# Low bits of all weight tiles by a 16-bit shift on VectorE, the first chunk's remainders on POOL, four rebiases on ScalarE, and a new order for the first part

## The chip, the cores and the metric

One core of one Trainium2 chip. The metric is the time of one execution in device microseconds (us). A core has TensorE (PE in the profile; PEld is its weight load), VectorE (DVE), ScalarE (ACT), GpSimd (POOL) and SyncE (SP, which issues nearly all transfers). Each engine works through its own queue in order and waits on semaphores for the others.

## The reference

A block attention followed by a gated feed-forward layer, in fp32.

```python
# 8 batches, 8 heads, 512 local and 32 global tokens, head size 64
s_g = scale * q_g @ [k_g, k_l].T;  out_g = softmax(s_g) @ [v_g, v_l]
# a local token sees the 32 global keys and local keys within 32 places
out_l = softmax([scale * q_l @ k_g.T, masked scale * q_l @ k_l.T]) @ [v_g, v_l]
x = concat(out_g, out_l), heads side by side          # 8 * 544 rows of 512
xn = x / sqrt(mean(x * x) + 1e-6) * rms_g
g = xn @ w_gate;  val = xn @ w_val                    # 512 x 1536 each
out = (g * sigmoid(g) * val) @ w_out                  # 1536 x 512
```

The kernel's weights arrive as float64: the host passes each as pairs of 32-bit words, a low and a high one, and the kernel makes fp32 of them on the chip.

## The kernel before

The tokens go through in nine chunks: chunks 0 to 7 are the 512 local rows of a batch, chunk 8 the 256 global rows. A matmul in full precision is made of three fp16 products: a value is split into a high half (its rounding to fp16) and a low half (the remainder), and high by high, high by low and low by high are summed. Chunks 0 and 1 compute attention unit by unit (two heads each, units 0 to 3 for chunk 0 and 4 to 7 for chunk 1); from chunk 2 on the weights are used in a folded form that chunk 1 writes to device memory.

Everything up to chunk 1's first product of the layer is the "first part": all of chunk 0, chunk 1's attention, and the preparation of all weights. Its order is written out by hand in the string `ORDER`, a list of jobs. A job is a letter, a number and sometimes an index; it issues its instructions on its engines, and the order of the list is the order of each engine's queue. What comes later (chunks 1 to 8) is ordered by loops with slots.

The jobs that matter here, with the number of the unit, tile or f behind the letter:

- Attention of a unit: `L` and `V` load, `S` scores (TensorE), `M` masked least value (VectorE, from PSUM), `E` exponentials (ScalarE), `T` transposes (TensorE), `C` copies (ScalarE), `A` values (TensorE), `R` reciprocal and `X` division (VectorE), `Q` squares (ScalarE), `Z` their sums (VectorE).
- Norm of a chunk: `N` 13 small steps (VectorE), `D` four diagonal factors `dg` (VectorE, L888), `U` transposed and scaled rows (TensorE), `H` their high half (ScalarE), `Y` their low half (VectorE).
- Weight tile i (0 to 11 are tiles of w_gate and w_val, 12 to 17 of w_out, two blocks f each): `W` load of two raw tiles `wr`, `m` rebias of the high word (VectorE for the tiles of `MULT_V`, else ScalarE), `s` shift by 3 (VectorE), then the three low bits: `l` (VectorE, ORed into the tile) or, for the tiles of `LOW_A`, `k` (ScalarE, into the low half of the raw high word), `g` sign and, after `k`, these bits (VectorE), `q` squares (ScalarE). `p` and `e` make scales of a group of tiles (TensorE, VectorE), `a` is the high half (ScalarE), `d` the low half (VectorE). `K0` to `K2` make the scales of w_out, which `a12` and the later ones need.
- Layer of chunk 0, block f: `I` four products (TensorE), `B` tanh (ScalarE), `b` gate and `h` inner product (VectorE, from PSUM), `c` the high half of the result (ScalarE), `r` its remainder (`low` in `first_chunk`). `Oi.j` are the output products of blocks 2i and 2i+1 for rows j, `o` the store. `J`, `j`, `u` fold a tile for the later chunks.

Since the banks of PSUM for I's two halves are single, I of block f+1 starts when `b` (and for its second half `h`) of block f is done.

Of the kernel before, what the change touches and what calls it, by code (L numbers as in the profile page):

```python
# [11 lines left out]
F16 = mybir.dt.float16  # L12
BF16 = mybir.dt.bfloat16
I32 = mybir.dt.int32
U32 = mybir.dt.uint32
I16 = mybir.dt.int16
AF = mybir.ActivationFunctionType
ALU = mybir.AluOpType
AX = mybir.AxisListType
# [3 lines left out]
P = 128  # L23
# [15 lines left out]

ORDER = """  # L40

L0 L1 L2 L3 W0 W1 V0 V1 S0 z0 V2 V3 z1 M0.0 W2 M0.1 S1 E0.0 W3 z2 W4 E0.1 T0.0 W5 M1.0 z3 W6
M1.1 S2 C0.0 L4 R0 E1.0 z4 L5 T0.1 m0 W7 E1.1 M2.0 T1.0 z5 M2.1 S3 C0.1 R1 s0 E2.1 m1 T1.1 M3.0
E2.0 M3.1 A0 z6 E3.1 R2 s1 l0 V4 C1.0 C1.1 X0 T2.0 E3.0 g0 A1 l1 Q0 T2.1 C2.0 V5 X1 T3.0 C2.1
R3 Z0 Q1 T3.1 g1 q0 A2 Z1 q1 p0 X2 C3.0 p1 C3.1 e0 Q2 A3 m2 e1 Z2 a0 s2 X3 k2 d0 m3 Q3 g2 m4 Z3
q2 s3 N0.0 k3 s4 N0.1 N0.2 N0.3 N0.4 N0.5 N0.6 N0.7 N0.8 a1 g3 k4 N0.9 d1 W8 S4 N0.10 N0.11
N0.12 q3 D0 L6 g4 U0.0 m5 M4.0 U0.1 H0.0 s5 q4 Y0.0 U0.2 M4.1 H0.1 k5 Y0.1 U0.3 I0.00 H0.2 g5
H0.3 I0.10 Y0.2 q5 W9 Y0.3 p2 m6 m7 I0.01 e2 k6 s6 I0.11 s7 l7 p3 B0 a2 b0 W10 e3 a3 I1.00 W11
h0 a4 d2 I1.01 c0 a5 d4 I1.10 B1 r0 m8 I1.11 b1 d5 m9 I2.00 h1 m10 d3 I2.10 c1 k9 g6 I2.01 r1
I2.11 g7 B2 q6 b2 W12 s9 q7 I3.00 h2 g9 c2 I3.10 k10 r2 I3.01 s8 m11 I3.11 B3 l8 k11 p4 b3 g8  # L50
I4.00 W13 e4 q8 I4.01 h3 a6 s11 I4.10 s10 B4 d6 q9 I4.11 c3 b4 a7 r3 I5.00 h4 d7 c4 I5.10 E4.1
r4 I5.01 g10 I5.11 g11 B5 q10 p5 b5 q11 m12 I6.00 h5 m13 e5 I6.10 c5 s12 a8 r5 I6.01 l12 k13
I6.11 d8 p6 B6 g12 a9 b6 W14 q12 d9 I7.00 W15 E4.0 h6 I7.01 e6 c6 s13 a10 I7.10 r6 B7 g13 m14
I7.11 b7 W16 q13 d10 I8.00 m15 h7 I8.01 s14 c7 s15 a11 I8.10 r7 l15 B8 m16 I8.11 b8 k14 s16
I9.00 h8 g15 I9.10 c8 g14 k16 W17 I9.01 r8 I9.11 d11 B9 q14 T4.0 b9 T4.1 g16 q15 I10.00 h9 m17
S5 R4 q16 s17 I10.01 L7 M5.0 c9 I10.10 M5.1 B10 C4.0 r9 C4.1 I10.11 b10 E5.1 l17 I11.00 E5.0
h10 A4 g17 c10 I11.01 R5 q17 X4 V6 r10 Q4 I11.10 K0 B11 Z4 b11 K1 I11.11 K2 a12 T5.0 h11 T5.1
S6 C5.0 d12 C5.1 c11 A5 M6.0 a13 O0.0 M6.1 V7 E6.0 X5 O0.1 d13 Q5 T6.0 E6.1 r11 O0.2 Z5 O0.3
a14 R6 C6.0 T6.1 d14 S7 C6.1 O1.0 a15 M7.0 M7.1 E7.0 O1.1 d15 O1.2 E7.1 T7.0 O1.3 a16 R7 T7.1
d16 A6 O2.0 X6 C7.0 C7.1 Q6 A7 a17 Z6 O2.1 X7 d17 Q7 O2.2 Z7 G J0 j0 u0 O2.3 N1.0 N1.1 N1.2  # L60
N1.3 N1.4 O3.0 N1.5 N1.6 N1.7 N1.8 N1.9 N1.10 O3.1 N1.11 N1.12 D1 J1 j1 u1 J2 j2 u2 O3.2 O3.3
O4.0 O4.1 O4.2 O4.3 O5.0 O5.1 o0 U1.0 o1 O5.2 H1.0 Y1.0 U1.1 o2 O5.3 H1.1 Y1.1 U1.2 o3 U1.3
H1.2 Y1.2 H1.3 Y1.3
"""


# [1 line left out]
def attention_moe_kernel(  # L68
# [17 lines left out]
    nc = tc.nc  # L86
# [20 lines left out]
    def f32(ap):  # L107
        return ap.bitcast(F32)
# [28 lines left out]
    ends = con.tile([P, 1], I32, tag="ends", name="ends")  # L137
# [16 lines left out]
    def sub(eng, dst, a, b):  # L154
        if eng == "V":
            nc.vector.tensor_tensor(dst, a, b, ALU.subtract)
        else:
            nc.gpsimd.tensor_tensor(dst, a, b, ALU.subtract)  # L158
# [31 lines left out]
    g2 = con.tile([P, 2], F32, tag="g2", name="g2")  # L190
# [47 lines left out]
    def convert(i):  # L238

        src = w_in[i] if i < NF else w_out[i - NF]  # L240
        raws = []
        t = []

        def load():
            for w in range(2):
                raw = raw_tile(RAW[i], f"wr{i}{w}")
                QW.dma_start(raw, src[:, w, :].bitcast(I32))
                r = raw.rearrange("p (n t) -> p n t", t=2)
                raws.append((slice(w * 512, (w + 1) * 512), r[:, :, 0], r[:, :, 1], raw))

        def rebias():

            t.append(
                xg.rearrange("p k n -> p (k n)").bitcast(I32)
                if i == NF - 1
                else raw_tile("wo" if i >= NF else "wf", f"w{i}t")
            )
            t32[i] = f32(t[0])
            for c, _, hi, _ in raws:
                if i in MULT_V:  # L260
                    nc.vector.tensor_single_scalar(f32(t[0][:, c]), f32(hi), REBIAS, ALU.mult)
                else:
                    nc.scalar.mul(f32(t[0][:, c]), f32(hi), REBIAS)

        def shift():
            nc.vector.tensor_single_scalar(t[0], t[0], 3, ALU.logical_shift_left)

        def three():

            for _, lo, _, raw in raws:  # L270
                half = raw.bitcast(I16).rearrange("p (n t) -> p n t", t=4)
                nc.scalar.activation(  # L272
                    half[:, :, 2],
                    lo.bitcast(U32),
                    AF.Copy,
                    bias=-0.5 + 7.5 * 2.0**-18,
                    scale=(1 - 2.0**-18) * 2.0**-29,
                )

        def low():  # L280
            for c, lo, _, _ in raws:
                nc.vector.scalar_tensor_tensor(
                    t[0][:, c], lo, 29, t[0][:, c], ALU.logical_shift_right, ALU.bitwise_or
                )

        def sign():

            keep = ends if i in LOW_A else -(1 << 30)
            for c, _, hi, _ in raws:
                nc.vector.scalar_tensor_tensor(  # L290
                    t[0][:, c], hi, keep, t[0][:, c], ALU.bitwise_and, ALU.bitwise_or
                )
# [993 lines left out]
    def first_chunk():  # L1286
        ch = chunks[0]
        ps, ts = {}, {}
# [348 lines left out]
```

## Time and profile before

| | |
|---|---|
| median of 3 runs | 933.66 us (933.59 to 934.74) |
| profiled execution, first to last instruction | 930.2 us |
| what lies around it, by the median | 3.5 us |
| busy: PE, VectorE, ScalarE, POOL | 893.9, 634.0, 495.4, 253.8 us |
| chunk 1's first product | 170.73 us |
| TensorE idle up to there | 28.8 us |

The page gives no separate time for the profiled execution beside its span; the median stands for it. A row of a timeline is the start, the duration, the engine, the line, the instruction and its operands (out<-in), a count where like rows follow each other, and in brackets the idle time before it with what ended it. The durations of one engine's instructions overlap a little, so costs are taken from start to start.

### The profile page before, as it was taken

The page shows a single profiled execution, that of the slowest core. Times are in us where ns is not written, and L with a number is a line of the kernel's source. Part 1 is how long each engine was busy: PE and PEld are TensorE (multiplying, and loading weights), DVE is VectorE, ACT ScalarE, POOL GpSimd, SP SyncE. Part 2 cuts the span into 40 slices and gives each one's busy share as a digit, 9 for nine tenths or more (in the row PEclk, how much of TensorE's full clock was granted, in tenths as well). Part 3 has the DMA queues.
Part 4 walks back from the last instruction along what each step waited for, and adds up shares of the span by engine and source line. Part 5 has one row for each costly group of instructions (what it writes and reads, how often), then busy time and mean ns, then how long its engine had stood idle before and what let it go on. Part 6 is the DMA issues. An engine that isn't in the chain of part 4 may idle for free.

```text
span 930.2 us, 26398 instructions
## 1 busy us (share of the span) xinstructions
PE 893.9 (96%) x11028; PEld 612.2 (66%) x11028; DVE 634.0 (68%) x1603; ACT 495.4 (53%) x1232; POOL 253.8 (27%) x219
## 2 busy tenths in 40 slices
PE   5489999999999999999999999999999999999998
PEld 4444455545447885688648874788568865886584
DVE  6999987887884588557775679357846774664331
ACT  6999994555443564456344655356445732543131
POOL 0000000142423262334332353236233432332020
PEclk9699999999999999999999999999999999999999
DMA  9972533686449854495609771685349632787000
GB/s 352 407 288 96 159 120 115 209 265 198 144 119 320 282 180 147 133 299 169 213 24 279 242 238 43 200 279 184 139 136 297 190 95 79 248 273 238 35 1 23
DMA packets 83495, 173.40 MB, mean 186 GB/s; under 512 B 6705, under 2 KB 25393, under 8 KB 83377
## 3 DMA queue, kind: packets, MB, share of 16 engines
q1 hardware_dynamic: 82944, 171.40, 56.1%
q8 instruction: 86, 1.41, 0.6%
q10 hardware_dynamic: 432, 0.33, 0.1%
q14 instruction: 33, 0.26, 0.1%
HBM read 150.21 MB, written 21.50 MB: 185 GB/s over the span
## 4 chain that ended last, share of the span: by engine, by line
PE 82%; DVE 8%; DMA 4%; ACT 3%; issue 1%; POOL 1%; ACTq 0%; DVEq 0%; POOLq 0%
PE pq L1108 36%; PE po L1266 23%; PE p L1205 9%; PE a L708 4%; PE po L1333 3%; PE s L665 3%; DMA k<-in_qk_dram 2%; DMA v<-in_vw_dram 1%; DMA wr<-in_w_in_dram 1%; PE ga L838 1%; PE gs L781 1%; PE gt L824 1%; DVE wf L373 1%; ACT wr L272 1%; DVE t L1302 1%
## 5 line engine op out<-in xcount | busy, mean ns | idle before, releaser
L1108 PEld LDWEIGHTS <-wt 128*128 128x128 f16 x3024 | 292.6, 98 | 40.9 <-issue 5.3
L1266 PE MATMUL po<-wo,h 128*128 128x512 f16 x1080 | 236.2, 379 | 0.0
L1108 PE MATMUL pq<-xh,wt 128*128 128x256 f16 x1152 | 204.3, 273 | 0.0
L1266 PEld LDWEIGHTS <-h 128*128 128x128 f16 x1080 | 105.2, 98 | 123.9 <-issue 1.0
L1108 PE MATMUL pq<-xl,wt 128*128 128x256 f16 x576 | 157.0, 273 | 0.0
L1108 PE MATMUL pq<-ht,wt 128*128 128x256 f16 x1296 | 155.6, 273 | 0.9 <-issue 0.9
L642 POOL TENSOR_TENSOR e<-e,sm 128x512 f32<-128x512 f32 x48 | 50.0, 1042 | 291.4 <-DVE sm L641 287.6
L158 POOL TENSOR_TENSOR h<-t,h 128x512 f16<-128x512 f32 (+1 forms) x90 | 102.4, 1145 | 95.1 <-ACT h L1248 54.2
L1205 PE MATMUL p<-xh,wf 128*128 128x512 f16 x384 | 119.4, 382 | 6.9 <-DVE t L1302 6.3
L1205 PEld LDWEIGHTS <-wf 128*128 128x128 f16 x576 | 55.9, 99 | 74.4 <-issue 12.4
L1140 POOL TENSOR_TENSOR s<-s,s 128x512 f32<-128x512 f32 x36 | 48.2, 1339 | 190.6 <-ACT s L1137 117.9
L627 ACT ACTIVATE e<-e,sm 128x128 f32<-128x128 f32 x192 | 75.2, 393 | 36.6 <-DVE sm L613 36.5
L1170 ACT CAST h<-t 128x512 f16<-128x512 f32 x72 | 44.4, 616 | 57.3 <-DVE t L1162 56.7
L1205 PE MATMUL p<-xl,wf 128*128 128x512 f16 x192 | 73.5, 383 | 0.0
L1162 DVE SCALAR_TENSOR_TENSOR t<-t,c_h,v 128x512 f32<-128x512 f32 x72 | 70.7, 989 | 0.0
L1151 ACT ACTIVATE t<-u,half_inv 128x512 f32<-128x512 f32 x72 | 48.1, 715 | 38.7 <-DVE u L1126 28.6
L1126 DVE TENSOR_TENSOR v<-pq,s 128x512 f32<-128x512 f32 x72 | 49.6, 689 | 24.5 <-PE pq L1108 23.8
L1139 DVE TENSOR_TENSOR s<-pq,s 128x512 f32<-128x512 f32 x36 | 24.9, 691 | 44.3 <-PE pq L1108 42.2
L1133 ACT COPY s<-pq 128x512 f32<-128x512 f32 x36 | 21.0, 584 | 51.3 <-PE pq L1108 51.3
L613 DVE CUSTOM_DVE_ANT_0 e<-s,maskb 128x128 f32<-128x128 f32 x192 | 45.8, 278 | 2.8 <-PE s L665 2.8
L1126 DVE TENSOR_TENSOR u<-pq,s 128x512 f32<-128x512 f32 x36 | 24.9, 691 | 32.9 <-PE pq L1108 24.5
L1158 DVE SCALAR_TENSOR_TENSOR t<-t,u 128x512 f32<-128x512 f32 x72 | 46.9, 679 | 0.5 <-ACT t L1151 0.5
(352 smaller groups left out, 1281.5 us busy)
## 6 DMA issues: line engine op xcount, KB each, us to landing
wt<-wd SPq DMA_DIRECT2D x120, 512.0 KB, 4.8
wr<-in_w_in_dram SPq DMA_DIRECT2D x24, 512.0 KB, 9.9
k<-in_qkb_dram SPq DMA_DIRECT2D x24, 448.0 KB, 6.6
gkq<-in_gkq_dram SPq DMA_DIRECT2D x16, 576.0 KB, 6.5
wt<-wd SPq DMA_DIRECT2D x36, 256.0 KB, 4.7
out_dram<-o SPq DMA_DIRECT2D x34, 256.0 KB, 2.1
v<-in_vb_dram SPq DMA_DIRECT2D x24, 352.0 KB, 7.1
v<-in_vw_dram SPq DMA_DIRECT2D x16, 512.0 KB, 9.7
```

The source lines that it names most:

```text
L158: nc.gpsimd.tensor_tensor(dst, a, b, ALU.subtract)
L613: nc.vector.tensor_tensor_reduce(out=e[:, g, :], in0=ps[:, g * P : (g + 1) * P], in1=late["mask"][:, m * P : (m + 1) * P], scale=-0.125, s ...
L627: nc.scalar.activation(e[:, g, :], e[:, g, :], AF.Exp, bias=sm[:, 0, j + g : j + g + 1], scale=-1.0, accum_out=sm[:, 1, j + g : j + g + 1],)
L642: nc.gpsimd.tensor_tensor(e, e, r.unsqueeze(2).to_broadcast([P, 4, P]), ALU.mult)
L1108: nc.tensor.matmul(ps[:, j * HT : (j + 1) * HT], w[:, j, i, k * P : (k + 1) * P], x[:, k * HT : (k + 1) * HT], start=first, stop=(p in end ...
L1126: nc.vector.tensor_tensor(o, ps, x.rearrange("p (j n) -> p j n", j=2), ALU.add)
L1140: nc.gpsimd.tensor_tensor(s(6), s(6), s(1), ALU.add)
L1151: nc.scalar.activation(t, st["u"][:, j, :], AF.Tanh, scale=half_inv[:, f : f + 1])
L1158: nc.vector.scalar_tensor_tensor(t, t, 1.0, u, ALU.add, ALU.mult)
L1162: nc.vector.scalar_tensor_tensor(t, t, c_h[:, f : f + 1], st["v"][:, j, :], ALU.mult, ALU.mult)
L1205: nc.tensor.matmul(ps[:, :n], rows[:, a, o : o + P], ch[z][k][:, :n], start=(k == 0 and i == 0), stop=(k == NK - 1 and i == 2),)
L1266: nc.tensor.matmul(ps[0], ch["h", f][:, a, j * P : (j + 1) * P], wo[f][:, z, :], start=(f == 0 and q == 0), stop=(f == NF - 1 and q == 2),)
```

## The change

Four things.

- The three low bits of every tile are now made by one VectorE pass over halfwords, `raw` seen as 16-bit numbers: the top halfword of the low word shifted right by 13, written over the low halfword of the high word. That is what ScalarE's `k` wrote. `k` is gone, `l` has a new content, and `g` masks with `ends` for all tiles.
- The rebias of tiles 3, 7, 11 and 12 goes from VectorE to ScalarE (`MULT_V`).
- The remainder `r` of chunk 0 goes from VectorE to POOL.
- `ORDER` is a new list of the same jobs, with `l` in place of `k`.

```diff
-    MULT_V = (0, 1, 3, 7, 11, 12)
-    LOW_A = (2, 3, 4, 5, 6, 9, 10, 11, 13, 14, 16)
+    MULT_V = (0, 1)
...
-        def three():
-            for _, lo, _, raw in raws:
-                half = raw.bitcast(I16).rearrange("p (n t) -> p n t", t=4)
-                nc.scalar.activation(
-                    half[:, :, 2],
-                    lo.bitcast(U32),
-                    AF.Copy,
-                    bias=-0.5 + 7.5 * 2.0**-18,
-                    scale=(1 - 2.0**-18) * 2.0**-29,
+        def low():
+            for _, _, _, raw in raws:
+                half = raw.bitcast(U16).rearrange("p (n t) -> p n t", t=4)
+                nc.vector.tensor_single_scalar(
+                    half[:, :, 2], half[:, :, 1], 13, ALU.logical_shift_right
                 )
-        def low():
-            for c, lo, _, _ in raws:
-                nc.vector.scalar_tensor_tensor(
-                    t[0][:, c], lo, 29, t[0][:, c], ALU.logical_shift_right, ALU.bitwise_or
-                )
...
-            keep = ends if i in LOW_A else -(1 << 30)
             for c, _, hi, _ in raws:
                 nc.vector.scalar_tensor_tensor(
-                    t[0][:, c], hi, keep, t[0][:, c], ALU.bitwise_and, ALU.bitwise_or
+                    t[0][:, c], hi, ends, t[0][:, c], ALU.bitwise_and, ALU.bitwise_or
                 )
...
-            sub("V", ch["h", f][:, 1, :], ts[f], ch["h", f][:, 0, :])
+            sub("P", ch["h", f][:, 1, :], ts[f], ch["h", f][:, 0, :])
...
-L0 L1 L2 L3 W0 W1 V0 V1 S0 z0 V2 V3 z1 M0.0 W2 M0.1 S1 E0.0 W3 z2 W4 E0.1 T0.0 W5 M1.0 z3 W6
+L0 S0 z0 M0.0 M0.1 E0.0 z1 z2 L1 S1 z3 E0.1 T0.1 T0.0 M1.0 E1.0 C0.0 M1.1 z4 R0 L2 S2 L3 M2.0 W0
```

Three places in the queues, with `w3t` the tile being built, `wr` its raw tiles, `wf` its halves, `rn` and `ss` the norm's small tiles, `t` and `h` chunk 0's result and its halves, `p` the products in PSUM. Behind the change the lines of the file stand up to 16 lower in number: L290 is L275, L266 is L263, L373 is L357, L888 is L872, L1302 and L1305 are L1286 and L1289, L156 (VectorE) and L158 (POOL) are `sub`, on POOL now L156. L268 is the new shift.

VectorE's queue around chunk 0's diagonal factors, before:

```order
L290 SCALAR_TENSOR_TENSOR w3t<-wr_238,ends,w3t 128x512
L290 SCALAR_TENSOR_TENSOR w3t<-wr_240,ends,w3t 128x512
L926 SCALAR_TENSOR_TENSOR rn_103<-rn_103 128x4
L373 SCALAR_TENSOR_TENSOR wf_717<-w1t,ws_676,wf_717 128x1024
L924 TENSOR_TENSOR rn_103<-rn_103 128x4
L925 SCALAR_TENSOR_TENSOR rn_103<-rn_103 128x4
L926 SCALAR_TENSOR_TENSOR rn_103<-rn_103 128x4
L888 TENSOR_SCALAR dg_768<-ident,rn_103 128x128 x4
L290 SCALAR_TENSOR_TENSOR w4t<-wr_250,ends,w4t 128x512
L290 SCALAR_TENSOR_TENSOR w4t<-wr_252,ends,w4t 128x512
```

and now:

```order
L908 TENSOR_TENSOR rn_103<-rn_103 128x4
L909 SCALAR_TENSOR_TENSOR rn_103<-rn_103 128x4
L268 TENSOR_SCALAR wr_529<-wr_529 128x512
L268 TENSOR_SCALAR wr_531<-wr_531 128x512
L910 SCALAR_TENSOR_TENSOR rn_103<-rn_103 128x4
L263 TENSOR_SCALAR w3t<-w3t 128x1024
L872 TENSOR_SCALAR dg_688<-ident,rn_103 128x128 x4
L268 TENSOR_SCALAR wr_683<-wr_683 128x512
L268 TENSOR_SCALAR wr_685<-wr_685 128x512
L357 SCALAR_TENSOR_TENSOR wf_662<-w0t,ws_584,wf_662 128x1024
```

The sign passes of w2t and w3t and the low half of tile 0 (`wf_662<-w0t`) now stand behind `dg`, and between the norm's steps stand the short shifts instead.

VectorE's queue in the middle of chunk 0's products, before:

```order
L156 TENSOR_TENSOR h_961<-t_921,h_961 128x512
L1302 SCALAR_TENSOR_TENSOR t_973<-t_973,p_1_940 128x512
L373 SCALAR_TENSOR_TENSOR wf_963<-w5t,ws_930,wf_963 128x1024
L1305 SCALAR_TENSOR_TENSOR t_973<-t_973,c_h,p_1_966 128x512
L373 SCALAR_TENSOR_TENSOR wf_938<-w3t,ws_883,wf_938 128x1024
L290 SCALAR_TENSOR_TENSOR w6t<-wr_276,ends,w6t 128x512
L290 SCALAR_TENSOR_TENSOR w6t<-wr_278,ends,w6t 128x512
L156 TENSOR_TENSOR h_961<-t_973,h_961 128x512
```

and now:

```order
L357 SCALAR_TENSOR_TENSOR wf_1197<-w6t,ws_1131,wf_1197 128x1024
L268 TENSOR_SCALAR wr_1065<-wr_1065 128x512
L268 TENSOR_SCALAR wr_1067<-wr_1067 128x512
L1286 SCALAR_TENSOR_TENSOR t_1225<-t_1225,p_5_1179 128x512
L268 TENSOR_SCALAR wr_903<-wr_903 128x512
L268 TENSOR_SCALAR wr_905<-wr_905 128x512
L1289 SCALAR_TENSOR_TENSOR t_1225<-t_1225,c_h,p_5_1206 128x512
L275 SCALAR_TENSOR_TENSOR w9t<-wr_903,ends,w9t 128x512
L275 SCALAR_TENSOR_TENSOR w9t<-wr_905,ends,w9t 128x512
L357 SCALAR_TENSOR_TENSOR wf_1242<-w7t,ws_1131,wf_1242 128x1024
```

The remainders (`h<-t,h`) have left VectorE's queue; shifts (L268), signs (L275) and low halves (L357) follow the inner product (L1289).

POOL's queue now begins with what VectorE gave up; before, it began with the division of chunk 2's attention (`e<-e,sm`):

```order
L156 TENSOR_TENSOR h_806<-t_770,h_806 128x512
L156 TENSOR_TENSOR h_806<-t_895,h_806 128x512
L156 TENSOR_TENSOR h_1060<-t_974,h_1060 128x512
L156 TENSOR_TENSOR h_1060<-t_1040,h_1060 128x512
L156 TENSOR_TENSOR h_1204<-t_1093,h_1204 128x512
L156 TENSOR_TENSOR h_1204<-t_1225,h_1204 128x512
```

Twelve of them stand there, one for each block f, each behind ScalarE's `c` of its block.

More of the change, by code (lines that the diff above doesn't have):

```diff
@@ L14 @@
 I32 = mybir.dt.int32
-U32 = mybir.dt.uint32
-I16 = mybir.dt.int16
+U16 = mybir.dt.uint16
 AF = mybir.ActivationFunctionType
@@ L40 @@
 ORDER = """
-L0 L1 L2 L3 W0 W1 V0 V1 S0 z0 V2 V3 z1 M0.0 W2 M0.1 S1 E0.0 W3 z2 W4 E0.1 T0.0 W5 M1.0 z3 W6
[L43 to L63, printed above, removed]
+L0 S0 z0 M0.0 M0.1 E0.0 z1 z2 L1 S1 z3 E0.1 T0.1 T0.0 M1.0 E1.0 C0.0 M1.1 z4 R0 L2 S2 L3 M2.0 W0
+M2.1 T1.0 m0 s0 S3 C0.1 l0 M3.1 E1.1 R1 g0 T1.1 V0 A0 X0 E2.1 E2.0 R2 C1.0 C1.1 Q0 W1 T2.0 M3.0 z5
@@ new lines @@
+E3.1 T2.1 V1 A1 E3.0 V2 C2.0 C2.1 T3.1 V3 m1 l1 s1 g1 X1 Q1 R3 Z0 Z1 z6 W2 W3 T3.0 q0 A2 X2 p0 e0
+q1 p1 e1 C3.0 C3.1 Q2 Z2 A3 X3 a1 d1 Q3 Z3 N0.0 N0.1 N0.2 N0.3 N0.4 a0 m2 N0.5 N0.6 l2 N0.7 N0.8
+N0.9 s2 N0.10 N0.11 m3 l3 N0.12 W4 s3 D0 U0.0 m4 l4 d0 H0.0 W5 m5 s4 g2 U0.1 H0.1 U0.2 H0.2 U0.3
+H0.3 q2 W6 m6 Y0.0 Y0.1 Y0.2 L4 I0.00 Y0.3 I0.01 B0 g3 q3 l5 b0 W7 W8 m7 I0.10 g4 I0.11 h0 q4 c0
+s5 I1.00 p2 e2 a2 S4 M4.0 I1.01 m8 g5 B1 d2 b1 L6 W9 I1.10 I1.11 l7 q5 M4.1 L5 h1 a3 m9 s8 s7 d3
+r0 I2.00 I2.01 c1 r1 I2.10 V7 I2.11 B2 b2 s6 p3 e3 h2 l8 g8 V4 E4.1 E4.0 a5 I3.00 I3.01 a4 d4 B3
@@ new lines @@
+b3 I3.10 g7 I3.11 q8 h3 c2 r2 l6 W10 m10 W11 c3 g6 q7 I4.00 I4.01 B4 d5 r3 s10 q6 b4 I4.10 I4.11
+p4 e4 S5 M5.1 I5.00 I5.01 m11 s11 h4 s9 a6 d6 E5.1 c4 I5.10 W12 I5.11 l10 B5 b5 I6.00 I6.01 r4 a7
+l9 h5 I6.10 g9 W13 I6.11 m12 d7 m13 c5 B6 b6 q9 g10 q10 L7 h6 r5 c6 l11 g11 I7.00 s13 I7.01 B7
+I7.10 b7 q11 p5 e5 T4.0 l13 r6 a8 d8 C4.0 a9 I7.11 g13 q13 h7 d9 p6 T4.1 e6 I8.00 I8.01 C4.1 c7
+s12 B8 b8 l12 g12 a10 I8.10 I8.11 h8 W14 I9.00 m14 s14 d10 W15 W16 m15 q12 I9.01 B9 b9 c8 r7 a11
+l14 I9.10 I9.11 h9 c9 g14 I10.00 d11 s15 I10.01 B10 q14 I10.10 I10.11 m16 b10 I11.00 I11.01 r8 l15
@@ new lines @@
+A4 r9 M5.0 E5.0 h10 W17 m17 I11.10 c10 B11 l16 g15 s17 s16 l17 g17 q15 T5.0 C5.0 V5 T5.1 C5.1 q17
+I11.11 S7 g16 A5 R4 R5 X4 q16 K0 M7.1 K1 K2 Q4 Z4 a12 d12 a13 b11 h11 c11 S6 M6.0 E6.0 O0.1 r10
+d13 M6.1 a17 d17 r11 E6.1 a14 X5 Q5 O0.0 M7.0 d14 R6 Z5 a15 d15 O0.3 O1.3 O0.2 O1.1 O1.2 O1.0 O2.1
+O2.2 a16 d16 O3.2 E7.0 E7.1 J0 j0 O4.2 O3.1 R7 T6.0 T6.1 u0 V6 T7.0 T7.1 C6.0 C6.1 A6 O2.3 C7.0
+C7.1 A7 J1 X6 Q6 X7 Q7 G Z6 Z7 N1.0 O5.2 N1.1 j1 N1.2 N1.3 N1.4 O2.0 o2 O3.0 O4.0 O5.0 o0 N1.5
+N1.6 N1.7 N1.8 N1.9 N1.10 N1.11 N1.12 D1 u1 U1.0 U1.1 J2 U1.2 U1.3 H1.0 H1.1 j2 Y1.0 Y1.1 O3.3
@@ L64 @@
+O4.3 u2 H1.2 H1.3 Y1.2 Y1.3 O4.1 O5.1 o1 O5.3 o3
 """
@@ L302, in squares @@
                 )
-        third = ("k", three) if i in LOW_A else ("l", low)
-        for n, fn in (("W", load), ("m", rebias), ("s", shift), third, ("g", sign), ("q", squares)):
+        for n, fn in zip("Wmslgq", (load, rebias, shift, low, sign, squares)):
             job[f"{n}{i}"] = fn
```

## The prediction

> **What bounds the kernel now.** I read the page first, then the busy time in five stretches, then who TensorE waited for, and last the timeline of VectorE around the joints.
>
> ```profile
> span 930.2 us, 26398 instructions
> DVE  6999987887884588557775679357846774664331
> POOL 0000000142423262334332353236233432332020
> PEclk9699999999999999999999999999999999999999
> ...
> 0.00:31.71 31.71, 20.80 (x570) 16.12 (x570) 21.34 (x117) 23.50 (x88) 0.20 (x4) 0.95 0.96 366
> 31.71:44.57 12.86, 2.06 (x66) 1.71 (x66) 12.45 (x36) 12.86 (x16) 0.00 (x0) 0.53 1.03 405
> 44.57:129.80 85.23, 78.31 (x628) 40.90 (x628) 82.64 (x184) 81.09 (x145) 0.00 (x0) 0.97 0.51 178
> 129.80:170.73 40.93, 40.80 (x442) 23.21 (x441) 31.41 (x89) 23.17 (x61) 0.00 (x0) 1.00 0.31 100
> 170.73:930.20 759.47, 751.88 (x9328) 530.22 (x9325) 486.21 (x1182) 354.79 (x927) 253.59 (x215) 1.00 0.57 181
> ...
> PE p L1205 <- DVE t L1302: 6.3, 6, 2.5
> PE p L1205 <- DVE t L1305: 0.6, 2, 0.4
> ```
>
> The rows of stretches give length, then busy time of PE, PEld, DVE, ACT and POOL. From 170.73 on TensorE works 751.88 of 759.47 us, and the change does not touch what is issued there: I take that part as fixed. The first part, up to 170.73, has three stretches. To 44.57 the first attention and the first weights are prepared. From 44.57 to 129.80 VectorE works 82.64 of 85.23 us: it is the bound, and ScalarE with 81.09 comes close behind. TensorE's only waits of that stretch are for VectorE, 6.3 and 0.6 us. From 129.80 on TensorE is full again. POOL stands still through all of it (0.00).
>
> ```profile
> 30.36 1.35 PE L537 MATMUL a<-v,pt 128*32 128x64 f32 x64
> 42.51 1.96 PE L479 MATMUL s<-k,q 64*32 64x128 f32 x64 [10.80 <-DMA k<-in_qk_dram]
> 43.69 0.88 DVE L888 TENSOR_SCALAR dg<-ident,rn 128x128 f32<-128x128 f32 x4
> 128.39 1.41 DVE L394 SCALAR_TENSOR_TENSOR wo<-w12t,hs,wo 128x512 f16<-128x512 f32 x2
> 130.86 2.76 PE L1333 MATMUL po<-wo,h 128*128 128x512 f16 x12
> 170.73 0.38 PE L1205 MATMUL p<-xh,wf 128*128 128x512 f16 x1
> 13.36 0.41 DVE L261 TENSOR_SCALAR w0t<-wr 128x512 f32<-128x512 f32 x1
> 14.97 0.43 DVE L261 TENSOR_SCALAR w0t<-wr 128x512 f32<-128x512 f32 x1 [1.20 <-DMA wr<-in_w_in_dram]
> 29.54 0.69 DVE L548 TENSOR_TENSOR x<-a,sm 128x512 f32<-128x512 f32 x1 [0.92 <-PE a L537]
> ```
>
> These are the joints: `dg` (job D0) ends at 44.57, the low half of the first w_out tile (d12) at 129.80, the first output product O0.0 starts at 130.86, chunk 1 at 170.73. The 10.80 us in front of S4 at 42.51 is a load that TensorE's queue meets before U0; D0 is not ready earlier in any case.
>
> **The change part by part.** The prices, as VectorE's and ScalarE's queues show them (start to start, so a pair of 1.29 is two times 0.60 and a tail):
>
> ```profile
> 56.12 1.29 DVE L282 SCALAR_TENSOR_TENSOR w7t<-wr,w7t 128x512 int32<-128x512 int32 x2
> 57.34 0.68 DVE L1302 SCALAR_TENSOR_TENSOR t<-t,p 128x512 f32<-128x512 f32 x1
> 66.29 1.41 DVE L290 SCALAR_TENSOR_TENSOR w6t<-wr,ends,w6t 128x512 int32<-128x512 int32 x2
> 67.61 0.69 DVE L156 TENSOR_TENSOR h<-t,h 128x512 f16<-128x512 f32 x1
> 68.22 1.29 DVE L290 SCALAR_TENSOR_TENSOR w7t<-wr,w7t 128x512 int32<-128x512 int32 x2
> 53.07 0.75 DVE L261 TENSOR_SCALAR w7t<-wr 128x512 f32<-128x512 f32 x2
> 53.74 0.15 DVE L177 TENSOR_SCALAR pow<-nrm 128x2 int32<-128x2 int32 x1
> L272 ACT ACTIVATE wr<-wr 128x512 int16<-128x512 uint32 x22 | 27.5, 1377 | 0.0
> 54.11 2.49 ACT L272 ACTIVATE wr<-wr 128x512 int16<-128x512 uint32 x2
> 52.98 1.23 ACT L263 ACTIVATE w6t<-wr 128x512 f32<-128x512 f32 x2
> ```
>
> An old low pass costs VectorE 1.20 a tile (7 tiles), the sign pass with `ends` 1.32 against 1.20 without, a rebias there 0.67, a remainder (L156) 0.60. The new shift is not in the trace. It reads and writes 512 halfwords, 8 bytes apart. Its nearest row is L261: also one input, 512 elements 8 bytes apart, 0.335 apiece. The far end is L282, 512 elements at 0.60. I take 0.335, so 0.67 a tile; the risk of 0.60 is a rival below. ScalarE loses 22 passes of 1.12 (24.6 us) and gains four rebiases of 1.13: 20 us less. That is worth nothing by itself, since VectorE with its 82.64 was ahead of it; it ends ScalarE as second bound.
>
> VectorE's content, with the jobs as the two orders place them:
> - Ahead of D0: out go d0 1.20, m3 0.67, g2 and g3 2.66, s4 0.60 (5.13); in come two shifts, l2 and l3 (1.34); l0 and l1 fall from 1.20 to 0.67 and g0, g1 rise by 0.12 each. Net -4.6.
> - D0 to d12: out go m7, m11, m12 (2.0), eleven remainders r0 to r10 (6.6), b11 and h11 (1.27); in come d0, g2, g3, s4 (4.46), nine shifts of tiles that ScalarE had done (6.03), M7.1 (0.85); five tiles trade 1.20 for 0.67 and get the dearer sign (-2.0). Net -0.5: 82.1 of work instead of 82.64.
>
> So the stretch that bounds hardly shrinks: what VectorE saves on remainders it spends on the tiles that ScalarE gave up and on work postponed from ahead of D0.
>
> D0's end: 44.57 - 4.6 = 39.97. The 1.20 wait for W0 goes, since three more score passes stand ahead of that rebias now; the 0.92 in front of the division goes too, since in the new queue e0 to Z2 come behind it. I grant 1.3 of these 2.1: D0 ends at 38.7. The values V0 to V3 hold no later place among the loads (V0 stands one weight tile earlier), A3, which started at 30.36, is followed by X3, Q3, Z3, and 13 root steps of 0.2 with two shifts, two s passes and D0 between (about 8 us): 38.7 is within reach of the data. S4's load no longer stands in front of U0. ScalarE's m4 ahead of H0.0 is hidden behind VectorE's d0 and g2.
>
> Now POOL. Its row and VectorE's in chunks where both work:
>
> ```profile
> L158 POOL TENSOR_TENSOR h<-t,h x12: 1156/1377/2141, 181.3 to 253.1; 128x512 f16<-128x512 f32 x12
> 344.62 1.16 POOL L158 TENSOR_TENSOR h<-t,h 128x512 f16<-128x512 f32 x1
> 344.67 1.67 DVE L1162 SCALAR_TENSOR_TENSOR t<-t,c_h,v 128x512 f32<-128x512 f32 x1
> L1162 DVE SCALAR_TENSOR_TENSOR t<-t,c_h,v x72: 737/746/1756, 299.3 to 850.6; 128x512 f32<-128x512 f32 x72
> 193.01 2.06 POOL L158 TENSOR_TENSOR h<-t,h 128x512 f16<-128x512 f32 x1 [0.81 <-ACT h L1248]
> 194.09 1.27 DVE L1055 TENSOR_TENSOR ws<-wq 128x256 f32<-128x256 f32 x1
> 195.39 0.42 DVE L1056 TENSOR_TENSOR ws<-ws,wq 128x256 f32<-128x256 f32 x1
> 190.79 0.65 DVE L1236 SCALAR_TENSOR_TENSOR t<-t,p 128x512 f32<-128x512 f32 x1
> 189.06 2.14 POOL L158 TENSOR_TENSOR h<-t,h 128x512 f16<-128x512 f32 x1
> ```
>
> A remainder alone takes POOL 1.16. While it runs, a VectorE instruction with two inputs in SBUF stands: L1162 took 1.67 instead of 0.74 (+0.93, up to 1.01 in the 72), L1055 1.27 instead of 0.42 (+0.85). One that reads PSUM does not: L1236 took 0.65 inside the POOL instruction of 189.06. And POOL, when it comes second, waits for VectorE (2.06 to 2.14) and goes next. The shifts, s passes, sign passes and low halves make three quarters of VectorE's queue from D0 to d12; signs and low halves have two SBUF inputs. Each of the eleven remainders starts some 0.5 us behind its h pass, when ScalarE has rounded; in the new queue nine of them meet s, l, g or d there, and two (r0, r8) meet score or gate passes from PSUM. Nine by 0.92 and two by 0.35 is 9.0 us. Bounds: 0 (all beside PSUM work) and 11 by 1.01 = 11.1. I take 9.0, near the upper end, since the queue is dense there.
>
> [...]
>
> The sum: d12 ends at 38.7 + 82.1 + 9.0 + waits. VectorE waited 2.6 in the old stretch (85.23 - 82.64); 0.8 of it for ScalarE's low pass goes, and TensorE runs ahead of a later VectorE: 1.5. That gives 131.3, against 129.80. The old O0.0 stood 1.06 behind d12 for other reasons (the A5 product); the new O0.1 needs only d12's first half, 0.66 before its end: 130.7 against 130.86. From there TensorE needs what it needed, 39.87, plus 0.4 for O1.3, which is up before d13's first half, plus about 0.7 for a slow clock after the idle time ahead of O0.1 (the row 31.71:44.57 shows 0.53 granted with an idle TensorE). Chunk 1 starts at 171.7, 1.0 later: span 931.2. The profiled span of 930.2 lies 3.5 under the median of 933.66; with the same 3.5 the time is 934.7. In the tail r10 and r11 on POOL are due at O5 only; D1 with its 13 root steps ends about 1 us before TensorE reaches U1.0, behind O2 to O5, which hide it.
>
> **Rivals.**
> - POOL's remainders cost VectorE little, because they fall beside gates and score passes. For it: PSUM readers were never slowed. Against: only a quarter of the queue is of that kind. With no loss d12 ends at 38.7 + 82.1 + 1.5 = 122.3, or some 1.5 later because TensorE's own 78.31 us then stands close behind VectorE and each waits for the other: O0.1 at about 123.2, less the clock's 0.7, is 7 earlier than the forecast, 927.5. With half the loss 930. The break-even is 0.73 us a remainder; 0.27 for being faster by over 1.9.
> - [...] Chance 0.26.
> - The shift does not run two elements a step: 0.60 instead of 0.335. Then 28 shifts of the bound stretch and 8 ahead of it cost 0.265 more each, 9.5 us: 944. For it: its elements are halfwords with gaps, which no row shows. Against: L261's gaps of the same 8 bytes. Chance 0.10. [...]
>
> **How the numbers follow.** The forecast, lead and lock cancelling to within 0.2% (1.9 us, about what a measurement here tells from no change), has 0.37; the faster rival 0.27; the slower two 0.26 and 0.10. So faster 0.27, same 0.37, slower 0.36. The forecast's own range is 931.8 to 935.6. Half of the faster cases lie above 929 (half of the loss taken), and the lock rival ends at 938; the slow shift is left outside: 928.5 to 938.5 leaves out about 2 in 10.
>
> **What would show it.** D0 ending near 38.7 shows the lead. Shift rows of about 0.42 at 0.335 apart (0.68 at 0.60 would be the third rival). Sign passes and low halves of 1.6 us and more beside POOL's L156 rows, summing to about 9 us. TensorE idle for some 5 us ahead of O0.1, ended by `wo` or K2. Chunk 1's first product near 171.7. It is wrong if remainders cost under 0.5 or if VectorE waits for ScalarE or the loads more than 2 us between D0 and d12.

## The result, and the profile after

The changed kernel takes 944.4 us, the median of 4 runs (942.54 to 947.46), against 933.62 of before: a ratio of 1.011, 95% interval 1.0092 to 1.0128. It is slower by 1.1%, where 934.7 and a range to 938.5 were forecast. The profiled execution took 942.54, 1.8 more than its span.

From the page of the changed kernel, the span and the busy tenths of a slice (VectorE, POOL, TensorE's clock):

```profile
span 940.7 us, 26398 instructions
...
DVE  5999998788876677656784579467756774664331
...
POOL 0012120042323343323532253235333432233020
PEclk9599999999999999999999999999999999999999
```

POOL now works in the first slices, VectorE's nines fill five slices (of 23.5 us) instead of four, and TensorE's granted clock in the second slice is 0.5 where it was 0.6. The stretches, cut where before's were (31.71, the end of `dg`, the end of d12, chunk 1's first product); columns as in the prediction:

```profile
0.00:31.71 31.71, 21.04 (x507) 17.16 (x508) 20.96 (x111) 22.45 (x86) 0.20 (x4) 0.84 0.97 369
31.71:42.74 11.03, 2.46 (x69) 2.22 (x67) 10.46 (x38) 6.55 (x10) 0.00 (x0) 0.50 1.03 406
42.74:141.05 98.31, 86.19 (x814) 45.42 (x813) 97.06 (x197) 70.28 (x136) 17.89 (x11) 0.93 0.52 172
141.05:180.90 39.85, 39.85 (x319) 21.48 (x318) 33.53 (x84) 24.53 (x61) 1.15 (x1) 0.96 0.24 80
180.90:940.70 759.80, 751.57 (x9327) 530.25 (x9325) 484.71 (x1179) 353.94 (x926) 253.19 (x215) 1.00 0.57 181
```

The joints themselves, from the timelines of VectorE and TensorE:

```profile
41.87 0.87 DVE L872 TENSOR_SCALAR dg<-ident,rn 128x128 f32<-128x128 f32 x4
139.62 1.42 DVE L378 SCALAR_TENSOR_TENSOR wo<-w12t,hs,wo 128x512 f16<-128x512 f32 x2
140.34 1.04 PE L1317 MATMUL po<-wo,h 128*128 128x512 f16 x2
180.93 0.38 PE L1189 MATMUL p<-xh,wf 128*128 128x512 f16 x1
```

Chunk 1 starts at 180.93 instead of 170.73, 10.2 later, and what follows it takes 759.80 against 759.47: all of the loss is in the first part, as the prediction has it for any effect. Of the 10.2, the stretch from `dg` to d12 gives 13.1 (98.31 against 85.23), while the lead ahead of it gives back only 1.8 (42.74 against 44.57) and what lies between d12 and chunk 1 another 1.1 (39.85 against 40.93). VectorE is busy 97.06 of the 98.31, where an instruction that is held off by POOL counts as busy: VectorE bounds the stretch, and it hardly waits for another engine's results. The rows of the shift, grouped, and one pair with the instruction behind it:

```profile
L268 DVE TENSOR_SCALAR wr<-wr 128x512 uint16<-128x512 uint16 x36 | 26.1, 832 | 0.0
61.05 1.32 DVE L268 TENSOR_SCALAR wr<-wr 128x512 uint16<-128x512 uint16 x2
62.16 0.32 DVE L477 CUSTOM_DVE_ANT_0 e<-s,mask 128x128 f32<-128x128 f32 x1
```

A pair takes 1.11 from its start to the next start, so 0.555 an instruction. The prediction took 0.335.

### The profile page after: what moved, and what is told of

It reads as the page before. It is cut to its first block, busy times and chain, and to the rows that moved or that the text cites. A ratio compares the mean times of both kernels' runs of the same rounds, so it can differ in the third digit from the quotient of the medians.

```text
span 940.7 us, 26398 instructions
## 1 busy us (share of the span) xinstructions
PE 901.1 (96%) x11028; PEld 616.5 (66%) x11028; DVE 646.7 (69%) x1605; ACT 477.7 (51%) x1218; POOL 272.4 (29%) x231
## 4 chain that ended last, share of the span: by engine, by line
PE 82%; DVE 10%; DMA 5%; ACT 1%; issue 1%; POOL 1%; SPq 0%; ACTq 0%; DVEq 0%; POOLq 0%
PE pq L1092 36%; PE po L1250 23%; PE p L1189 9%; PE a L692 4%; PE po L1317 4%; DMA wr<-in_w_in_dram 3%; PE s L649 3%; DVE wr L268 2%; DVE wf L357 1%; DMA v<-in_vw_dram 1%; PE ga L822 1%; PE gs L765 1%; PE gt L808 1%; DVE t L1289 1%; DMA k<-in_qk_dram 1%
## 5 line engine op out<-in xcount | busy, mean ns | idle before, releaser
L156 POOL TENSOR_TENSOR h<-t,h 128x512 f16<-128x512 f32 (+1 forms) x102 | 121.1, 1193 | 220.1 <-ACT h L1297 124.8
L1124 POOL TENSOR_TENSOR s<-s,s 128x512 f32<-128x512 f32 x36 | 48.1, 1336 | 190.7 <-ACT s L1121 118.0
L1110 DVE TENSOR_TENSOR v<-pq,s 128x512 f32<-128x512 f32 x72 | 49.6, 689 | 24.2 <-PE pq L1092 23.5
## 6 DMA issues: line engine op xcount, KB each, us to landing
wr<-in_w_in_dram SPq DMA_DIRECT2D x24, 512.0 KB, 10.2
```

The costliest lines, as they stand in the source:

```text
L1110: nc.vector.tensor_tensor(o, ps, x.rearrange("p (j n) -> p j n", j=2), ALU.add)
L1124: nc.gpsimd.tensor_tensor(s(6), s(6), s(1), ALU.add)
```

## The experiments

Theory A: the halfword shift costs 0.555 and not 0.335 because its elements are halfwords with gaps, and VectorE sets the end of the first part, so its work counts one to one; POOL's remainders cost about what the prediction says. Theory B: the new order loses by its waits. Theory C: any pass over words or halfwords 8 bytes apart is that slow, the type has no part in it. Where the prediction and the expectations speak of a pace of one or two elements a step, the prices 0.555 to 0.60 and 0.335 are what was measured; such a pace in steps no run shows. Beside them, POOL's remainders may cost more, or nothing. In all kernels the median is compared with before's, run beside it (934.3 to 934.8). Differences between two changed kernels are those of their medians, most of them against the 943.56 of the first run below; before's medians differ by 0.5 from session to session.

**The changed kernel again**

> The changed kernel once more, beside the kernels below, so that all are compared with it under the same conditions. Every theory: 944 within 2 us.

943.56 us, ratio 1.0096 (1.0074 to 1.0118). It repeats. In its profile chunk 1 starts at 180.92.

**A shift of whole words**

```diff
-                half = raw.bitcast(U16).rearrange("p (n t) -> p n t", t=4)
-                nc.vector.tensor_single_scalar(half[:, :, 2], half[:, :, 1], 13, ALU.logical_shift_right)
+                nc.vector.tensor_single_scalar(lo, lo, 29, ALU.logical_shift_right)
```

> The shift of the three low bits is done as a 32-bit shift of the low word in place (512 words, 8 bytes apart, as in L261's rows) in place of the 16-bit one; the three bits are then not put into the weights. Theory A (the 16-bit shift goes one element a step, 0.555 us from start to start, where the prediction took 0.335, and VectorE sets the end of the first part): rows of L268 at 0.335 apart, 36 x 0.22 = 7.9 us saved, of which 1.8 ahead of dg; 944.4 - 7.9 = 936.5. Theory B (the loss is in the new order, whose waits would take the freed time up): rows may be shorter, but the time falls by less than 3: 941.5 or more. Theory C (any shift of strided words goes one element a step, the type has no part in it): rows stay at 0.555, 944.

935.15 us, ratio 1.0000 (0.9985 to 1.0015). The shift's rows and its stretches (same cuts, in this kernel's times):

```profile
L267 DVE TENSOR_SCALAR wr<-wr 128x512 int32<-128x512 int32 x36 | 15.0, 458 | 0.0
39.01 0.76 DVE L267 TENSOR_SCALAR wr<-wr 128x512 int32<-128x512 int32 x2
39.67 1.28 DVE L354 SCALAR_TENSOR_TENSOR wf<-w0t,ws,wf 128x1024 f16<-128x1024 f32 x1
```

```profile
39.09:132.85 93.76, 85.33 (x814) 46.12 (x813) 91.33 (x197) 70.37 (x136) 17.25 (x11) 0.94 0.57 196
132.85:171.65 38.80, 38.66 (x319) 21.15 (x318) 33.52 (x84) 24.42 (x61) 1.16 (x1) 1.00 0.25 82
171.65:935.10 763.45, 752.85 (x9327) 530.97 (x9325) 484.69 (x1179) 353.97 (x926) 253.14 (x215) 1.00 0.55 180
```

A pair takes 0.66, as priced, and the median is 8.4 below the changed kernel's 943.56, where 7.9 was priced: with the price of this one instruction the whole loss goes, and so does the miss. `dg` ends at 39.09 (38.7 forecast; 40.5 in the other kernel with the word shift, below) and chunk 1 starts at 171.65 (171.7 forecast). That this agrees so well is partly luck: d12 ends at 132.85, 1.5 behind the 131.3 of the forecast, and from the first output product (132.15) to chunk 1 it takes 39.5, 1.5 less than the 40.97 that the forecast counts there. (Behind chunk 1's start this execution took 763.45, 3.7 to 4.0 more than the executions profiled of the changed kernel and of before; its time, 936.9, is among the longest of its 12. So the joints are the finer measure.)

**The price by form**

The pass for the low bits in six forms, each `tensor_single_scalar` in place but for form 4, which multiplies and adds from `lo` into the low halfword of `hi`.

> A price list: the pass for the low bits in six forms, by tile number modulo 6, each 512 elements, results of most not what the kernel needs. 0: 16-bit shift in place, 8 bytes apart; 1: 32-bit shift in place, 8 bytes apart; 2: 16-bit, side by side; 3: 16-bit, 4 bytes apart; 4: multiply and add from unsigned 32-bit words to 16-bit halves, both 8 bytes apart; 5: 32-bit, side by side. Theory A (16-bit elements with gaps go one a step, words two a step): 0 and 3 start 0.555 apart, 1 and 5 0.335, 2 0.335 or less, 4 0.555. Theory C (the stride of 8 bytes does it): 0, 1 and 4 at 0.555; 2, 3 and 5 at 0.335.

One pair of each form, from VectorE's timeline of a single execution, in the order 0, 1, 2, 3, 4, 5, each with the row behind it:

```profile
16.78 1.35 DVE L289 TENSOR_SCALAR wr<-wr 128x512 uint16<-128x512 uint16 x2
17.92 0.33 DVE L496 CUSTOM_DVE_ANT_0 e<-s,mask 128x128 f32<-128x128 f32 x1
...
22.39 0.75 DVE L289 TENSOR_SCALAR wr<-wr 128x512 int32<-128x512 int32 x2
23.06 0.68 DVE L265 TENSOR_SCALAR w1t<-w1t 128x1024 int32<-128x1024 int32 x1
...
36.18 0.50 DVE L289 TENSOR_SCALAR wr<-wr 128x512 uint16<-128x512 uint16 x2
36.59 0.16 DVE L927 TENSOR_TENSOR rn<-rn 128x4 f32<-128x4 f32 x1
...
37.93 0.79 DVE L289 TENSOR_SCALAR wr<-wr 128x512 uint16<-128x512 uint16 x2
38.61 0.15 DVE L929 SCALAR_TENSOR_TENSOR rn<-rn 128x4 f32<-128x4 f32 x1
...
40.07 1.31 DVE L273 TENSOR_SCALAR wr<-wr 128x512 int16<-128x512 uint32 x2
41.16 1.26 DVE L376 SCALAR_TENSOR_TENSOR wf<-w0t,ws,wf 128x1024 f16<-128x1024 f32 x1
...
49.16 0.75 DVE L289 TENSOR_SCALAR wr<-wr 128x512 int32<-128x512 int32 x2
49.91 0.69 DVE L1305 SCALAR_TENSOR_TENSOR t<-t,p 128x512 f32<-128x512 f32 x1
```

Start to start, for one instruction of 512 elements: halfwords 8 bytes apart 0.57; words 8 bytes apart 0.335; halfwords side by side 0.205; halfwords 4 bytes apart 0.34; from words to halfwords, both 8 bytes apart, 0.545; words side by side 0.375 at most. Neither theory had it whole: halfwords with gaps can be as fast as words (form 3, against A), and the 8 bytes alone do not hinder (form 1, against C). What the two slow forms share is an operand of halfwords 8 bytes apart, so with a step of four of its own elements; with a step of two elements, or one, all forms are fast (0.205 to 0.375, against 0.545 and 0.57). No form has a step of four words, so whether the count of elements decides, or halfwords 8 bytes apart alone are slow, stays open. Form 4 also differs from the others in what it computes and in changing the type, so it does not show by itself that a wide step of the output is enough. A step of four halfwords costs 0.57 here and 0.555 in the changed kernel, where a step of two costs 0.34.

**The remainders back on VectorE**

```diff
-            sub("P", ch["h", f][:, 1, :], ts[f], ch["h", f][:, 0, :])
+            sub("V", ch["h", f][:, 1, :], ts[f], ch["h", f][:, 0, :])
```

> The changed kernel with chunk 0's remainders back on VectorE. Theory A (POOL's remainder holds VectorE off any instruction whose inputs come from SBUF; in the changed kernel eleven rows are longer by 9.4 us in sum): 9.4 of stalls go, eleven remainders of 0.60 come back (6.6), 2.8 earlier: 941.6. Rival (the long rows stand beside waits that remain): nothing is won and 6.6 of work comes: 947 to 951.

939.29 us, ratio 1.0042 (1.0025 to 1.0059): 4.3 less than the changed kernel, more than the 2.8 expected. The 1.5 between them is as large as the spread of `dg`'s end between executions (below). POOL's remainders lose. The stretch from `dg` to d12 with them on VectorE:

```profile
41.73:136.20 94.47, 84.63 (x814) 45.12 (x813) 93.47 (x206) 70.18 (x136) 0.00 (x0) 0.95 0.54 184
```

The stretch is 3.8 shorter. The rows that show the stall are the changed kernel's, first three instructions without POOL, then the same kinds beside it (from VectorE's timeline):

```profile
59.26 1.28 DVE L357 SCALAR_TENSOR_TENSOR wf<-w2t,ws,wf 128x1024 f16<-128x1024 f32 x1
71.03 1.39 DVE L275 SCALAR_TENSOR_TENSOR w8t<-wr,ends,w8t 128x512 int32<-128x512 int32 x2
77.02 1.34 DVE L268 TENSOR_SCALAR wr<-wr 128x512 uint16<-128x512 uint16 x2
...
64.91 2.18 DVE L357 SCALAR_TENSOR_TENSOR wf<-w3t,ws,wf 128x1024 f16<-128x1024 f32 x1
74.13 2.31 DVE L275 SCALAR_TENSOR_TENSOR w7t<-wr,ends,w7t 128x512 int32<-128x512 int32 x2
88.06 2.29 DVE L268 TENSOR_SCALAR wr<-wr 128x512 uint16<-128x512 uint16 x2
```

and POOL's own, at the same times:

```profile
64.51 1.50 POOL L156 TENSOR_TENSOR h<-t,h 128x512 f16<-128x512 f32 x1 [7.56 <-ACT h L1297]
74.18 1.70 POOL L156 TENSOR_TENSOR h<-t,h 128x512 f16<-128x512 f32 x1 [8.18 <-ACT h L1297]
87.08 2.08 POOL L156 TENSOR_TENSOR h<-t,h 128x512 f16<-128x512 f32 x1 [7.83 <-ACT h L1297]
```

Each of the eleven remainders lengthens one VectorE row: by 0.89, 0.92, 0.91, 0.94, 0.98, 0.94, 0.88, 0.71, 0.42, 0.92 and 0.95, in the order of time. The sum is 9.46 us.

**Both edits**

> Both edits at once: the low word shifted in place as 32-bit words (bits not put in), the remainders on VectorE. Theory A: the two sums add up, 944.4 - 7.9 - 2.8 = 933.7, the time of before within 2 us; nothing is left of the loss. If another engine takes over as the bound on the way, 935 to 937. Rival B (the new order itself loses): 938 or more.

932.26 us, ratio 0.9969 (0.9957 to 0.9982), chunk 1 at 169.66. That is 11.3 less than the changed kernel's 943.56, where the two edits by themselves gave 8.4 and 4.3: they add up but for 1.4. With the word shift the remainders' move is worth 2.9, the size that the rows give (9.46 - 6.6). It is 0.3% faster than before, but without the three bits.

**The remainders twice on POOL**

```diff
-            sub("P", ch["h", f][:, 1, :], ts[f], ch["h", f][:, 0, :])
+            for _ in range(2):
+                sub("P", ch["h", f][:, 1, :], ts[f], ch["h", f][:, 0, :])
```

> The changed kernel with each remainder of chunk 0 computed twice on POOL, the second over the first. It doubles the suspected cost and leaves VectorE's own work as it is. Theory A: each second instruction holds VectorE off once more: 11 x 0.86 = 9.4 later, 953. Rival (one pause of VectorE covers both, or POOL runs beside it): 944 to 946.

950.32 us, ratio 1.0169 (1.0145 to 1.0192): 6.8 more than the changed kernel. Its stretch from `dg` to the first output product:

```profile
41.25:146.99 105.74, 87.79 (x812) 45.96 (x811) 103.94 (x197) 70.33 (x136) 35.32 (x22) 0.90 0.50 166
```

VectorE issues what it issued, and what its rows take beyond their usual time sums to 16.89 us in this stretch, against 9.46. The second instructions cost 0.68 each (7.43 by eleven), not 0.86: some find no row there to lengthen (the pair of 54.31, 2.41 long, lengthens a step of the scales by 0.89; beside its second instruction stand score passes with their usual 0.28, and the sign pass behind them takes 0.08 more). So POOL's instructions themselves hold VectorE off.

**One part alone: the remainders on POOL, all else as before**

> The kernel before with one part of the change alone: chunk 0's remainders on POOL. Theory A (each remainder on POOL holds VectorE off by 0.86 us, the mean of the eleven in the changed kernel, where its own 0.60 on VectorE was cheaper): 11 x 0.26 = 2.8 later, 937.5. Rival (in this order the remainders fall beside reads of PSUM): up to 6.6 earlier, 928 to 932.

935.25 us, ratio 1.0003 (0.9988 to 1.0017): no change, between the two expectations. Here nine of the eleven remainders meet a row that they lengthen, by 7.4 us in sum, 0.8 more than the 6.6 that the eleven remainders of 0.60 free. (The profiled execution took 937.18, the second longest of its 12; in it chunk 1 starts at 173.51, 2.8 behind before's. The median of the 12 is the better measure.) What a remainder on POOL costs here depends on what stands beside it in the order: nothing for two of these eleven, 0.42 to 0.98 each in the changed kernel.

**One part alone: the low bits by the shift, all else as before**

> The kernel before with one part of the change alone: the low bits of all tiles by the 16-bit shift on VectorE, where ScalarE's passes and VectorE's ORed passes stood; order, remainders and rebiases as before. Theory A (the new pair of shift and sign pass costs VectorE 1.11 + 1.32 = 2.43 a tile, as much as the 1.20 + 1.20 = 2.40 that it replaces, so that the eleven tiles that ScalarE had done come on top): 3 of the eleven tiles fall ahead of dg (3.3), 8 behind it (8.9), 0.8 of waits for ScalarE go: dg near 48, the time 11.4 later, 945. Rival (the freed 25 us of ScalarE are worth something, since with 81 of 85 us it was as much a bound): half of it back, 939.

947.74 us, ratio 1.0143 (1.0123 to 1.0164). `dg` ends at 48.1 and the first output product starts at 142.59 instead of 130.86, 11.7 later, where 11.4 was expected; the median is 12.9 above before's. The stretch from `dg` to there:

```profile
48.12:142.59 94.47, 81.95 (x685) 43.58 (x683) 92.56 (x210) 64.19 (x126) 0.00 (x0) 0.94 0.44 148
```

VectorE is full with 92.56, and the room on ScalarE (64.19 busy) is worth nothing. By this part alone the change would have lost more than it did in the whole.

**One part alone: the new order**

> The kernel before with one part of the change alone: the new order. Low bits (eleven tiles on ScalarE, seven ORed in on VectorE), remainders and rebiases are as before, each at the place where the new order has its successor. Theory A (VectorE sets the end; against the changed kernel with remainders on VectorE, 939.3, it has nine shifts less behind dg, 10.0, and three rebiases more, 2.0): 931. Rival (with seven of the tiles on ScalarE the new order already lost to ScalarE's queue, 940.2): 938 to 943. In both the order by itself is told from before's 934.8.

944.80 us, ratio 1.0105 (1.0086 to 1.0124), slower than both expectations.

```profile
41.24:140.14 98.90, 83.63 (x813) 44.39 (x811) 85.54 (x193) 86.61 (x151) 0.00 (x0) 0.96 0.51 173
```

VectorE's work is what theory A counted (85.54), but it waits for 13.4 us. The waits are spread over many places, most of them for ScalarE:

```profile
DVE t L1301 <- ACT t L1298: 2.2, 2, 1.7
DVE xg L289 <- ACT wr L271: 2.1, 2, 1.7
DVE xl L903 <- ACT xh L899: 1.8, 2, 1.0
DVE wf L372 <- ACT wf L369: 1.6, 1, 1.6
```

With ScalarE's passes in it (86.61 busy) the new order loses by waits, while in the changed kernel it keeps VectorE waiting for 1.25 only. Order and split belong together. The fourth part, the four rebiases on ScalarE, was not run alone.

**Toward a faster kernel: low bits of some tiles on ScalarE, remainders on VectorE**

```diff
+            if i in LOW_A:   # ScalarE's old pass for these tiles
...
-            sub("P", ch["h", f][:, 1, :], ts[f], ch["h", f][:, 0, :])
+            sub("V", ch["h", f][:, 1, :], ts[f], ch["h", f][:, 0, :])
```

> The changed kernel with the remainders on VectorE and the low bits of five tiles (4, 7, 10, 13, 15) back on ScalarE, each at the place in the order where the shift stands. Theory A (VectorE sets the end, ScalarE has room): five times 1.11 less than with the remainders on VectorE alone (939.3): 933.7. Rival (ScalarE's passes of 2.25 a tile delay tanh and the high halves that TensorE and VectorE need): no gain, 939 to 941.

> As with five tiles, but seven (4, 5, 7, 10, 13, 14, 15). Theory A: 939.3 - 7 x 1.11 = 931.5 as long as VectorE sets the end; ScalarE would then work 70 + 16 = 86 of about 87 us between dg and the first output product, so 932 to 935 where it becomes a second bound. Rival: ScalarE is the bound already, slower than with five tiles, 936 to 941.

> The changed kernel with the remainders on VectorE and the low bits of six tiles on ScalarE, chosen by the room that its queue shows: 2 and 3 (ahead of dg, where it works 6 of 10 us), 7, 10, 13 and 16. Theory A (VectorE sets the end and ScalarE's passes stand where they delay nothing): 939.3 - 6 x 1.11 = 932.6, faster than before's 934.8. Rival (as with five tiles, where 1.7 of 5.5 was won: ScalarE's passes hold up tanh and the high halves): 936 to 938.

937.55 (ratio 1.0034, 1.0018 to 1.0049), 940.18 (1.0061, 1.0037 to 1.0085) and 940.29 (1.0059, 1.004 to 1.0079). None beats before. The stretch from `dg` to the first output product with five tiles, with seven, and with the six that were chosen by ScalarE's room:

```profile
41.57:134.00 92.43, 83.07 (x812) 44.12 (x811) 87.39 (x195) 77.72 (x144) 0.00 (x0) 0.96 0.55 188
```

```profile
41.73:136.67 94.94, 84.15 (x813) 44.38 (x812) 85.79 (x191) 81.99 (x148) 0.00 (x0) 0.95 0.54 181
```

```profile
40.68:136.12 95.44, 85.42 (x813) 46.55 (x811) 88.12 (x198) 79.47 (x147) 0.00 (x0) 0.93 0.53 180
```

With no tile on ScalarE (the remainders on VectorE alone, above) VectorE is busy 93.47 of 94.47 up to d12's end, and idle for 1.0. Counted to d12's end too, it is busy 88.54 of 93.58 with five tiles, 87.11 of 96.26 with seven and 89.45 of 96.77 with six: 4.9, 6.4 and 4.0 less work, and 5.0, 9.2 and 7.3 idle. Of this idle time 3.8, 7.0 and 6.4 are waits for ScalarE. So with five tiles most of the saved work comes back as waits, and with seven or six more than all of it. The choice by free share of ScalarE's time (six tiles) was a miss.

## Why the prediction was wrong

The step that failed is the price of the new shift, "I take 0.335, so 0.67 a tile", taken from L261 as the nearest row because its elements lie 8 bytes apart too. L261's elements are words, so these 8 bytes are two of its elements; they are four halfwords. The measured 0.555 is close to the far end, 0.60, and the rival that followed from it (944, at a chance of 0.10) is what happened: the sum below puts 1.8 + 6.2 = 8.0 of the miss down to it, and with a shift at 0.335 the time is before's. It stood at 0.10 although the text said that no row shows halfwords with gaps; the range was cut in front of it. An unshown price that counts 36 times deserved both ends in the range.

Point by point:

- *D0 at 38.7*: 42.74. Eight shifts ahead of it cost 8 x 0.22 = 1.8 of the 4.0. The rest is mostly the "1.3 of waits" that I granted: VectorE's idle time ahead of `dg` is 11.3, where it was 10.8, so 1.8 more than forecast. The 1.20 for W0 is gone, but the third score pass now waits 1.55, and the division of `a` 1.10 where it was 0.92:

```profile
14.91 0.29 DVE L477 CUSTOM_DVE_ANT_0 e<-s,mask 128x128 f32<-128x128 f32 x1 [1.55 <-PE s L463]
30.47 0.69 DVE L532 TENSOR_TENSOR x<-a,sm 128x512 f32<-128x512 f32 x1 [1.10 <-PE a L521]
```

  `dg`'s end also varies between executions: in four executions with the halfword shift and the same order up to there it was 41.25 to 42.74, where the third score's wait went from 0.82 to 1.56 and the division's from none to 1.10. The one that ends last, the changed kernel's at 42.74, was granted a TensorE clock of 0.84 up to 31.71, the one with the remainders on VectorE, at 41.73, 0.95; up to `dg`'s end it was 0.75 and 0.84, and 0.82 with the remainders twice, at 41.25, so it does not order the three.
- *Work from D0 to d12, 82.1*: 97.06 busy less 9.46 of stalls is 87.6. 28 shifts at 0.22 more are 6.2, which leaves 81.4. With the word shift it is 91.33 - 9.38 = 82.0. The count of instructions was right, one price wrong.
- *POOL's remainders, 9.0*: 9.46 by the rows. The size is right, and the reason given holds for instructions with two inputs in SBUF (six of the eleven rows, longer by 0.88 to 0.94). That it came out so closely is partly luck: the sum charged the one-input passes `s` and `l` with 0.92 as well, though its rows showed the stall for two inputs only, and in the run five of the eleven rows are one-input instructions (three shifts and two small steps of a group's scales) and are held off too, by 0.42 to 0.98. Of the two remainders that the forecast put beside PSUM work, r8 met a gate pass and then a shift (0.42), but r0 a step of the scales (0.89). The "lock" of the chances is shown by no run: what the runs show is VectorE rows longer by 0.42 to 0.98 beside POOL's remainders, 0.86 in the mean, so the rival that ends at 938 was too dear; the rival that hid them was wrong in this order, and in before's too (7.4 us).
- *Waits 1.5*: 98.31 - 97.06 = 1.25. *The output product 0.66 ahead of d12's end*: 140.34 against 141.05. *39.87 + 1.1 from there*: 40.59. *TensorE idle for some 5 us ahead of it*: 3.15, ended by VectorE's `kk` (L397) at 137.52, and then score products up to 140.34.
- *Fixed from chunk 1 on*: 759.80 against 759.47 in the profile that the sum was made for. Other executions took up to 763.45, so this part is fixed in its order, not to a microsecond.
- *The 3.5 between span and time*: it was 1.8 in the changed kernel's profiled execution and 1.8 to 2.4 in those of the experiments. By this, an estimate, before's profile shows an execution 1.1 to 1.7 faster than the median, and the 3.5 is not all time around the span. In the forecast it stands on both sides.

The sum with the measured terms: 38.7 + 1.8 + 2.2 for D0, then 82.1 - 0.7 + 6.2 of work, 9.5 of stalls, 1.25 of waits: 141.0.

What made the change lose, then: it replaced ScalarE's passes by VectorE's in the stretch that VectorE bounds. The pair of shift and sign pass costs 1.11 + 1.32 = 2.43 a tile, where the ORed pair cost 2.40, so nothing was saved on the seven tiles that VectorE had, and the shifts of eleven tiles came on top.

## What to carry to other kernels

For the price of a strided VectorE pass, look for a row with the same type and the same gap: a row with the same gap in bytes but another type is no neighbour (at 8 bytes, 0.555 for halfwords and 0.335 for words). Where an unknown price multiplies by dozens on the engine that bounds, let the range reach both ends of it, and ask what the new form costs against the one it replaces, pass by pass. Work moved to another engine "with room" pays only if the order lets it finish in time; its free share doesn't say so (with the six tiles chosen by that share VectorE had 4.0 less work and waited 6.4 for ScalarE).

## What was not expected of the hardware

- A one-input pass over 512 halfwords with a step of four took 0.555, with a step of two 0.34. A pass from words with a step of two to halfwords with a step of four took 0.545; it multiplies and changes the type as well.
- POOL also holds off some VectorE instructions with one input from SBUF. The word shift went from 0.76 to 1.73 a pair, and the halfword shift was longer by up to 0.98 a pair. Even an instruction of two elements a partition stood, here at 55.91 beside POOL's instruction of 55.79, against its usual 0.17:

```profile
55.91 1.06 DVE L334 TENSOR_SCALAR hs<-hs 128x2 int32<-128x2 int32 x1
...
68.98 0.17 DVE L334 TENSOR_SCALAR hs<-hs 128x2 int32<-128x2 int32 x1
```

  Not all are held off. In the trace of before a transpose with one SBUF input took its usual 0.70 wholly beside a POOL instruction:

```profile
235.72 1.16 POOL L158 TENSOR_TENSOR h<-t,h 128x512 f16<-128x512 f32 x1
235.91 0.70 DVE L647 STREAM_TRANSPOSE et<-e 128x512 f32<-128x512 f32 x1
```

  Reads of PSUM went on: the gate pass at 117.39 took 0.70 beside POOL's instruction of 117.38. What sets the one-input instructions that were held off apart from the transpose that was not, no run shows.
